# Attention's 64x64 products move from two tiles of the TensorE array to four

## The chip, the cores and the metric

The kernel runs on one core of one Trainium2 chip. The metric is the device time of that core in microseconds (us), from one launch, as the median of several runs. Five engines matter: PE is the matrix engine TensorE (PEld its weight loads), DVE VectorE, ACT ScalarE, POOL GpSimd, and SP issues the DMAs. PSUM is the memory into which TensorE writes. It has 8 banks of 128 partitions x 512 float32 values.

## The reference, cut to what matters

Attention runs inside chunks of 64 tokens, for 8 heads of dimension 64. Its output, with the heads put side by side, is the input of a gated layer, whose output is the input of a second layer.

```python
B, H, S, D = 8, 8, 576, 64           # 4608 tokens, H * D = 512 features
# q_c, k_c, v_c: (B, H, 9, 64, 64), chunks of 64 tokens
scores = np.matmul(q_c, k_c.transpose(0, 1, 2, 4, 3)) / np.sqrt(D)
attn = np.exp(scores - scores.max(-1)) ; attn /= attn.sum(-1) + 1e-09
x = np.matmul(attn, v_c)             # then (4608, 512)
y = (silu(x @ w_gate) * (x @ w_val)) @ w_out          # 512 -> 1536 -> 512
h = y @ w_in                                          # 512 -> 2048
out = (h * sigmoid(1.702 * h)) @ w_out2               # 2048 -> 512
```

## The kernel before, in words

**Tokens.** The 4608 tokens are 9 blocks of 512, and a block is 4 units of 128 tokens. A unit is two chunks of 64 tokens by 8 heads, so 16 small attention problems, 36 units in all.

**Passes.** Four passes go over the 9 blocks: two for the gated layer (half of its features each), two for the second layer. In pass 0 the attention of later units is computed between the products of the current block: while block b is multiplied, the attention of block b+1 is made ready. Units 0 to 3 come before everything else, units 4 to 7 go one by one (function `attend`), and units 8 to 35 are pipelined (`attend_next`): one PE step holds the value products of unit u-2 and then the score products of unit u.

**One unit.** `blocks` (L631) computes 16 products of 64x64 in float32, on 64 partitions each: rows 0 to 63 of the operands give rows 0 to 63 of the output, rows 64 to 127 give rows 64 to 127. Each such product stands in the trace as two pairs of a weight load and a matmul. So a set of 16 products is 32 pairs, and a unit has two sets, one for the scores (`s<-k,q`) and one for the values (`a<-e,v`). Between them stand the softmax (L670 the maximum, L671 the subtraction, both DVE reading the scores from PSUM; L673 the exponential on ACT; L674 to L678 sum and division on DVE) and four 128x128 transposes (L687), copied back by ACT (L690). `attended` copies the value products to `xr` (and, for block 0, also splits them into a high part and a low part, `x`, with ACT and DVE).

**Other products.** The layers multiply in three float32r matmuls each (`mm3`, L386 to L388), 128 rows by 128 columns with 256 or 512 moving columns. The first matrix product of a group is done in seven block products instead of eight, save in the first block (`group_plain`).

**PSUM.** The tags are `ya`, `yb` (two banks each) and `ga`, `gb`, `s`, `a` (one each), eight banks in all. `s` holds a unit's scores. `a` holds in turn its transposes and its value products. In pass 0 the products of the layers use `ga`, `gb`, `ya`, `yb`.

**Order.** No loop order decides what stands next to what: `Program` records every operation with a planned cost in us, a priority and its buffers, runs a list scheduler over them (with rounds that move priorities to due times) and emits the instructions of each engine in the order found. So a changed cost or dependency can move instructions anywhere. The weights come as 64-bit words and are converted on ACT and DVE (L456 to L464) and split (L370, L379) during pass 0, among them those of the later passes.

Of the kernel before, what the change touches and what calls it, by code (L numbers as in the profile page):

```python
# [20 lines left out]
P = 128  # L21
CH = 64
# [6 lines left out]
class Buf:  # L29
# [3 lines left out]
    def __init__(self, make, prev=None, before=None, whole=None):  # L33
        self.make, self.prev, self.before, self.whole, self.bank = make, prev, before, whole, False
        self.users, self.writers, self.openers, self.next, self.tile = [], [], [], None, None
# [18 lines left out]
class Ring:  # L54
    banks = None

# [3 lines left out]
    def new(self, shape, dtype=F32):  # L60
        def make():
            return self.pool.tile(shape, dtype, tag=self.tag, name=self.tag, bufs=self.bufs)

        prev = self.made[-self.bufs] if len(self.made) >= self.bufs else None
        b = Buf(make, prev, self.made[-1] if self.made else None)
        b.bank = self.pool is self.banks
        if prev is not None:
            prev.next = b
        self.made.append(b)
        return b  # L70
# [7 lines left out]
class Program:  # L78
# [15 lines left out]
    def op(self, eng, us, fn, reads=(), writes=(), prio=0, table=None, near=None, port=None):  # L94
# [7 lines left out]
        for b in writes:  # L102
            deps.update(b.users)
            if not b.users:
                if b.prev is not None:
                    deps.update(b.prev.users)
                    list(b.line())[-1].openers.append(o)
                if b.before is not None and b.before.tile is None:
                    follows.add(b.before.users[0])
        for b in (*reads, *writes):  # L110
            for a in b.line():
                a.users.append(o)
                for w in a.next.openers if a.next is not None else ():
                    w.deps.add(o)
                    w.follows.discard(o)
# [158 lines left out]
def attention_two_moe_kernel(ctx: ExitStack, tc: tile.TileContext, q, k, v, wg, wv, wo, wi, wo2, out):  # L274
# [51 lines left out]
    Ring.banks = pool["ps"]  # L326
    ring.update({tag: Ring(pool["ps"], tag, 1) for tag in ("ya", "yb", "ga", "gb", "s", "a")})
# [196 lines left out]
    def combos_from_quarters(j, g, prio):  # L524
# [3 lines left out]
        w3 = Buf(lambda: e.ap, e, None, e.whole)  # L528
# [110 lines left out]
    def unit(u, bufs=None, both=None):  # L639
# [3 lines left out]
        un.both = None  # L643
        if both is None:
            un.s = ring["s"].new([P, 512])
        else:
            un.both = ring[both].new([P, 2, 512])
            un.s = un.both.part(lambda ap: ap[:, 0])
        return un

    def in_a(un):
        return ring["a"].new([P, 512]) if un.both is None else un.both.part(lambda ap: ap[:, 1])

    def scores(un, prio, done=None):

        if done is None:
            op("pe", 1.24, lambda: blocks(un.s.ap, un.q.ap, un.k.ap), [un.q, un.k], [un.s], prio)
        else:
# [5 lines left out]
            attended(done, prio)  # L664

    def softmax(un, prio):
        s, e = un.s, un.e
        m = ring["m"].new([P, H, 1])
        z = ring["z"].new([P, H, 1])
        op("dve", 0.67, lambda: nc.vector.tensor_reduce(out=m.ap, in_=heads(s.ap), axis=AX.X, op=ALU.max), [s], [m], prio)  # L670
        op("dve", 0.68, lambda: nc.vector.tensor_tensor(  # L671
            out=heads(e.ap), in0=heads(s.ap), in1=m.ap.to_broadcast([P, H, CH]), op=ALU.subtract), [s, m], [e], prio)
# [8 lines left out]
    def turned(un, prio):  # L681
        pt, e = in_a(un), un.e
# [8 lines left out]
        un.o = in_a(un) if un.both is None else pt  # L691

    def attended(un, prio):
# [4 lines left out]
        if b == 0:  # L698
            n = un.u // 2
            if n not in X0:  # L700
                X0[n] = [ring["x"].new([P, KD, HT], F32R) for _ in range(2)]
            th = slice(un.u % 2 * P, un.u % 2 * P + P)
            split(*[x.part(lambda ap: ap[:, :, th]) for x in X0[n]], un.o, 512, prio, "dve",
                  lambda ap: ap.rearrange("p (a t) -> p a t", a=NP))
        copy(xr[b].part(lambda ap: ap[:, :, ts]), un.o, 512, prio, cut=lambda ap: ap.rearrange("p (a t) -> p a t", a=NP))

    def alone(un, prio):
        op("pe", 1.24, lambda: blocks(un.o.ap, un.v.ap, un.e.ap), [un.v, un.e], [un.o], prio, near=1.0)
# [108 lines left out]
    def group_products(g, xs, at, put, p):  # L817
# [3 lines left out]
        bank = [ring[t].new([P, 2, HT]) for t in (("s", "a") if p and n_groups[0] % 2 else ("ga", "gb"))]  # L821
# [33 lines left out]
    def group_plain(g, xs, at, put):  # L855
        n_groups[0] += 1
        bank = [ring[t].new([P, 2, HT]) for t in ("ga", "gb")]
# [44 lines left out]
    def group_gated(g, xs, at, put, early, apart):  # L902
# [61 lines left out]
        z = ring["ga"].new([P, 2, HT])  # L964
        bank = {label: ring[alone[label]].new([P, 2, HT]) if label in alone else z for label in ORDER[2]}
# [32 lines left out]
    def o_banks():  # L998
        ya, yb = [ring["y" + i].new([P, 2, 2, 256]) for i in "ab"]
        one = [ring[t].new([P, 2, 256]) for t in ("gb", "s", "a")]  # L1000
# [3 lines left out]
    def o_sum(p, b, label, banks, kept, prio):  # L1004
# [19 lines left out]
        m = banks[label]  # L1024
# [13 lines left out]
        elif label == "7":  # L1038
# [3 lines left out]
            if final:  # L1042
                tt(c, c, u3, ALU.add, 512, prio, "pool")
                tt(c, c, banks["5"], ALU.add, 512, prio)
            else:
                tt(c, u3, banks["5"], ALU.add, 512, prio)
            out_quarter(3, c)
            tt(u2, u2, banks["5"], ALU.add, 512, prio)
            tt(u3, u3, banks["4"], ALU.subtract, 512, prio)
# [38 lines left out]
    warm = ring["ya"].new([P, 2, 512])  # L1088
# [29 lines left out]
    for u in range(UPB):  # L1118
# [4 lines left out]
        attend(u, -40 + 4 * u, -60+3*u, bufs, (None, None, "yb", "ya")[u])  # L1123
# [166 lines left out]
```

## Time and profile before

| what | value |
|---|---|
| median of 3 runs | 1705.27 us (1704.3 to 1705.37) |
| the profiled execution's own time | 1703.92 us |
| its span in the profile | 1701.9 us |
| PE busy in the span | 1685.2 us (99%) |
| DVE, ACT, POOL busy | 1105.5, 887.1, 730.1 us |
| mean DMA rate | 278 GB/s |

The span runs from the first instruction of the program to the end of the last. About 2 us of the execution's time lie outside it. Busy time is the union of an engine's instructions. Matmuls overlap in the pipeline, so the distance from one start to the next says what a matmul costs, not its duration.

### The profile page before, as it was taken

To read this page: it belongs to the slowest core of one execution; us is meant where nothing else is said; L and a number is where in the kernel's file an instruction comes from. 1 tells how busy PE (TensorE), PEld (TensorE's weight loads), DVE (VectorE), ACT (ScalarE), POOL (GpSimd) and SP (SyncE) were. 2 spreads that over 40 slices of the span, in tenths; PEclk is the share of its full clock that TensorE was granted. 3 is DMA by queue.
4 is the path that set the end of the run, shared out by engine and by line. 5 is a ranking of instruction groups with operands and counts; after the bars stand their busy time and mean duration, and the time that the engine had idled before them with its cause. 6 is when DMAs were issued, how large, how long until landed. Compare 5 with 4: busy or idle time off the path is not lost.

```text
span 1701.9 us, 36408 instructions
## 1 busy us (share of the span) xinstructions
PE 1685.2 (99%) x14428; PEld 1609.8 (95%) x14428; DVE 1105.5 (65%) x1606; ACT 887.1 (52%) x1505; POOL 730.1 (43%) x736
## 2 busy tenths in 40 slices
PE   8999999999999999999999999999999999999998
PEld 7989999899999999999999999999999999999998
DVE  7878777787773664455454477887855556655555
ACT  7967766676643543333333456655544444444443
POOL 2595645565663464121211235667741133333333
PEclk9999999999999999999999999999999999999999
DMA  7668888888889988667779998999989977777773
GB/s 294 195 240 283 279 280 303 285 278 296 294 280 372 311 299 285 240 233 248 246 250 321 378 344 291 312 320 316 329 258 327 358 234 227 231 234 237 233 250 119
DMA packets 184154, 472.66 MB, mean 278 GB/s; under 512 B 19760, under 2 KB 44848, under 8 KB 183728
## 3 DMA queue, kind: packets, MB, share of 16 engines
q1 hardware_dynamic: 183984, 470.34, 81.2%
q8 instruction: 114, 1.87, 0.5%
q14 instruction: 56, 0.46, 0.1%
HBM read 331.84 MB, written 138.41 MB: 276 GB/s over the span
## 4 chain that ended last, share of the span: by engine, by line
PE 93%; DVE 2%; issue 1%; DMA 1%; ACT 1%; POOL 0%; POOLq 0%; DVEq 0%; ACTq 0%; SPq 0%
PE ga L386 11%; PE ga L388 11%; PE ga L387 11%; PE ya L386 5%; PE yb L388 5%; PE ya L388 5%; PE yb L386 5%; PE yb L387 5%; PE ya L387 5%; PE gb L386 4%; PE gb L388 4%; PE gb L387 4%; PE s L386 2%; PE s L388 2%; PE s L387 2%; PE a L386 2%
## 5 line engine op out<-in xcount | busy, mean ns | idle before, releaser
L370 ACT COPY u<-ga 128x512 f32<-128x512 f32 x222 | 129.8, 585 | 200.2 <-PE ga L388 199.3
L379 DVE TENSOR_TENSOR c<-u,ga 128x512 f32<-128x512 f32 x140 | 95.7, 684 | 173.2 <-PE ga L388 164.9
L386 PE MATMUL ga<-x,wc 128*128 128x256 f32 x728 | 207.7, 285 | 0.4
L387 PE MATMUL ga<-x,wc 128*128 128x256 f32 x728 | 205.5, 282 | 0.0
L388 PE MATMUL ga<-x,wc 128*128 128x256 f32 x728 | 205.4, 282 | 0.0
L924 ACT ACTIVATE xr<-c 128x512 f32<-128x512 f32 x136 | 86.0, 632 | 148.3 <-DVE c L379 146.8
L386 PEld LDWEIGHTS ga<-x,wc 128*128 128x128 f32 x728 | 138.3, 190 | 6.9 <-ACT u L370 3.1
L387 PEld LDWEIGHTS ga<-x,wc 128*128 128x128 f32 x728 | 138.5, 190 | 3.2
L388 PEld LDWEIGHTS ga<-x,wc 128*128 128x128 f32 x728 | 138.8, 191 | 0.0
L386 PE MATMUL ga<-x,wa 128*128 128x256 f32 x488 | 138.3, 283 | 0.0
L387 PE MATMUL ga<-x,wa 128*128 128x256 f32 x488 | 137.6, 282 | 0.0
L388 PE MATMUL ga<-x,wa 128*128 128x256 f32 x488 | 137.6, 282 | 0.0
L379 DVE TENSOR_TENSOR c<-u,gb 128x512 f32<-128x512 f32 x116 | 79.2, 682 | 87.7 <-ACT u L370 74.3
L379 POOL TENSOR_TENSOR u<-u 128x512 f32<-128x512 f32 x36 | 48.2, 1340 | 176.4 <-ACT u L370 176.4
L379 POOL TENSOR_TENSOR k<-xr,q 128x512 fp32r<-128x512 f32 x24 | 32.1, 1338 | 209.6 <-ACT q L370 181.2
L386 PE MATMUL ga<-x,wb 128*128 128x256 f32 x424 | 119.8, 283 | 0.6 <-ACT u L370 0.6
L388 PE MATMUL ga<-x,wb 128*128 128x256 f32 x424 | 119.7, 282 | 0.0
L387 PE MATMUL ga<-x,wb 128*128 128x256 f32 x424 | 119.6, 282 | 0.0
L379 DVE TENSOR_TENSOR xr<-xr 128x512 f32<-128x512 f32 x136 | 106.3, 782 | 11.1 <-ACT xr L924 9.2
L884 ACT ACTIVATE h<-c 128x512 f32<-128x512 f32 x102 | 63.8, 631 | 90.5 <-DVE c L379 87.8
L379 DVE TENSOR_TENSOR hl<-h,hh 128x512 fp32r<-128x512 f32 x108 | 84.6, 783 | 25.1 <-ACT hh L370 22.9
L379 DVE TENSOR_TENSOR h<-h,c 128x512 f32<-128x512 f32 x102 | 87.2, 858 | 20.9 <-ACT h L884 19.5
(335 smaller groups left out, 6224.3 us busy)
## 6 DMA issues: line engine op xcount, KB each, us to landing
x<-x_dram SPq DMA_DIRECT2D x182, 512.0 KB, 5.4
o<-od_b SPq DMA_DIRECT2D x119, 512.0 KB, 4.6
o<-od_a SPq DMA_DIRECT2D x102, 512.0 KB, 5.1
x_dram<-x SPq DMA_DIRECT2D x56, 512.0 KB, 5.4
wd_b<-ws SPq DMA_DIRECT2D x56, 256.0 KB, 4.4
od_b<-ws SPq DMA_DIRECT2D x56, 256.0 KB, 4.5
raw<-in_moe_w_out SPq DMA_DIRECT2D x44, 255.8 KB, 4.9
wd_a<-ws SPq DMA_DIRECT2D x42, 256.0 KB, 4.7
```

The lines of the kernel that those rows point to most:

```text
L370: op("act", act_us(n), lambda: nc.scalar.copy(out=dst.ap, in_=cut(src.ap)), [src], [dst], prio, near=near)
L379: lambda: e.tensor_tensor(out=dst.ap, in0=of_a(a.ap), in1=of_b(b.ap), op=by), [a, b], [dst], prio, near=near)
L386: nc.tensor.matmul(o, ah, bh, start=first, stop=False, **kind)
L387: nc.tensor.matmul(o, ah, bl, start=False, stop=False, **kind)
L388: nc.tensor.matmul(o, al, bh, start=False, stop=last, **kind)
L884: op("act", act_us(512), lambda h=h, i=i: nc.scalar.activation(out=h.ap, in_=of(0)(c[i].ap), func=AF.Silu), [c[i]], [h], prio, "silu")
L924: op("act", act_us(512), lambda: nc.scalar.activation(out=h.ap, in_=c.ap, func=AF.Gelu_apprx_sigmoid), [c], [h], prio, "gelu")
```

## The change

Four things change together.

- **Four tiles.** The 16 products of a set run over four combinations of operand rows (0 to 63, 64 to 127) and output rows (0 to 63, 64 to 127) instead of two. For the scores the operand rows are chosen by head parity and the output rows by the chunk. Products from different operand rows go to different banks, since both may write the same output rows. `score_blocks` and `value_blocks` go round the four tiles in the order (0,0), (1,1), (0,1), (1,0).
- **Banks.** The eight banks are one tile `banks`, cut by the class `Banks`, which tracks users bank by bank. A unit's scores take the left half (256 columns) of two banks, mostly those of `s` and `a`, and the value products of the unit before take the right half of the same two banks. The four transposes fill the second of the two banks, as before. In the first block unit 1 uses the banks of `ga` and `gb`.
- **Host layout.** The host lays q and k out by head parity, and permutes the rows of `w_gate` and `w_val` to match the new order of x's features. No work is added on the chip for that.
- **Planner.** The planned cost of one set falls from 1.24 to 0.8 us, that of two from 2.2 to 1.3, the time planned for attention in a block from 13 to 8 us, and units 4 to 7 get earlier priorities.

```diff
+class Banks:
+    HOME = {"ya": (0, 2), "yb": (2, 2), "ga": (4, 1), "gb": (5, 1), "gab": (4, 2), "s": (6, 1), "a": (7, 1), "sa": (6, 2)}
...
+        b = Buf(make, list(dict.fromkeys(a for a in self.last[first:first + n] if a is not None)))
...
-            t += sum(step_us(g) for g in gs) + (13.0 if p == 0 and b < NB - 1 else 0) + (3 * GV if p == b == 0 else 0)
+            t += sum(step_us(g) for g in gs) + (8.0 if p == 0 and b < NB - 1 else 0) + (3 * GV if p == b == 0 else 0)
...
-    def blocks(o, st, mv):
-        for i in range(H):
-            for r in (slice(0, CH), slice(CH, P)):
-                cs = slice(i * CH, i * CH + CH)
-                nc.tensor.matmul(o[r, cs], st[r, cs], mv[r, cs], start=True, stop=True)
+    def quads(places):
+        for g in range(H // 4):
+            for c in range(2):
+                for a, b in ((0, 0), (1, 1), (0, 1), (1, 0)):
+                    yield places(g, c, a, b)
+
+    def score_blocks(un):
+        for g, c, a, b in quads(lambda g, c, a, b: (2 * g + c, b, a, b)):
+            cs = h64(2 * g + b)
+            nc.tensor.matmul(un.s.ap[h64(b), a, h64(g)], un.q.ap[h64(a), cs], un.k.ap[h64(a), cs], start=True, stop=True)
+
+    def value_blocks(un):
+        for g, c, a, b in quads(lambda g, c, a, b: (g, c, a, b)):
+            cs = h64(2 * (2 * g + b) + c)
+            nc.tensor.matmul(un.o.ap[h64(b), a, h64(2 * g + c)], un.v.ap[h64(a), cs], un.e.ap[h64(a), cs],
+                             start=True, stop=True)
...
     def scores(un, prio, done=None):
+        t = two(un)
+        un.s = left(t)
         if done is None:
-            op("pe", 1.24, lambda: blocks(un.s.ap, un.q.ap, un.k.ap), [un.q, un.k], [un.s], prio)
+            op("pe", 0.8, lambda: score_blocks(un), [un.q, un.k], [un.s], prio)
         else:
+            done.o = right(t)
             def both_blocks():
-                blocks(done.o.ap, done.v.ap, done.e.ap)
-                blocks(un.s.ap, un.q.ap, un.k.ap)
-            op("pe", 2.2, both_blocks, [done.v, done.e, un.q, un.k], [done.o, un.s], prio, near=1.0)
+                value_blocks(done)
+                score_blocks(un)
+            op("pe", 1.3, both_blocks, [done.v, done.e, un.q, un.k], [done.o, un.s], prio, near=1.0)
...
-        pt, e = in_a(un), un.e
+        pt, e = two(un).part(lambda ap: ap[:, 1]), un.e
...
-            attend(UPB + u, t + 4 + u * 16, t - 6 + u * 16)
+            attend(UPB + u, t + 0 + u * 14, t - 10 + 0 + u * 14, None, "sa")
```

Three places show how the instructions moved. The first is PE's order at the program's start, with the score products of units 0 to 3 (L631 before, L662 now), the transposes (L687, L732), the value products (L667 now) and single matmuls on `ident` that only keep PE busy (L1096, L1146). Before:

```order
L631 MATMUL s<-k,q 64x64 x16
L1096 MATMUL ya<-ident 128x128 x6
L631 MATMUL yb<-hl,hh 64x64 x16
L631 MATMUL s<-hl,hh 64x64 x16
L1096 MATMUL ya<-ident 128x128 x4
L687 MATMUL a<-ident,e 128x128 x4
L1096 MATMUL ya<-ident 128x128 x10
L631 MATMUL a<-e,v 64x64 x16
L631 MATMUL ya<-hl,hh 64x64 x16
L631 MATMUL s<-k,q 64x64 x16
```

And now:

```order
L662 MATMUL banks<-k,q 64x64 x16
L1146 MATMUL banks<-ident 128x128 x2
L662 MATMUL banks<-hl,hh 64x64 x16
L1146 MATMUL banks<-ident 128x128 x2
L662 MATMUL banks<-hl,hh 64x64 x16
L1146 MATMUL banks<-ident 128x128 x10
L732 MATMUL banks<-ident,e 128x128 x4
L1146 MATMUL banks<-ident 128x128 x6
L667 MATMUL banks<-e,v 64x64 x16
L732 MATMUL banks<-ident,c 128x128 x4
```

The counts of products are the same. Units 1 and 2 still come early, but unit 4's scores (the last row of before) have moved behind the first products of the layer.

The second place is DVE in the same stretch, up to the second of the two subtractions that give the low part of x for units 2 and 3 (`x<-ya,x` before, the second `x<-banks,x` now); `t` and `wc` are weights under conversion, L678 and L723 the last step of unit 4's softmax. Before:

```order
L678 TENSOR_TENSOR e<-e,z 128x512
L379 TENSOR_TENSOR h<-h,gb 128x256
L461 SCALAR_TENSOR_TENSOR wc_365<-wc_365,wb_268 128x512 x2
L379 TENSOR_TENSOR h<-h,ga 128x256
L464 SCALAR_TENSOR_TENSOR wc_365<-wb_268,wc_365 128x512 x2
L379 TENSOR_TENSOR x<-yb,x 128x4x128
L461 SCALAR_TENSOR_TENSOR t<-t,wa_318 128x512
L464 SCALAR_TENSOR_TENSOR t<-wa_318,t 128x512
L379 TENSOR_TENSOR x<-ya,x 128x4x128
```

And now:

```order
L399 TENSOR_TENSOR h<-h,banks 128x256
L481 SCALAR_TENSOR_TENSOR wc_358<-wc_358,wb_273 128x512 x2
L484 SCALAR_TENSOR_TENSOR wc_358<-wb_273,wc_358 128x512 x2
L719 TENSOR_REDUCE z<-e 128x8
L720 TENSOR_SCALAR z<-z 128x8
L399 TENSOR_TENSOR x<-banks,x 128x4x128
L722 RECIPROCAL z<-z 128x8
L723 TENSOR_TENSOR e<-e,z 128x512
L399 TENSOR_TENSOR h<-h,banks 128x256
L481 SCALAR_TENSOR_TENSOR t<-t,wa_318 128x512
L484 SCALAR_TENSOR_TENSOR t<-wa_318,t 128x512
```

The second subtraction has moved ahead of the conversion of `t`, of the second `h` and of the end of unit 4's softmax.

The third place is DVE at a pipelined unit in block 2 of pass 0 (unit 13), between the maximum of its scores (L670, now L715) and the subtraction (L671, now L716), with the block sums `xt` of the next block's x between them. Before:

```order
L670 TENSOR_REDUCE m<-s 128x8
L379 TENSOR_TENSOR xt<-xr 128x512
L752 TENSOR_TENSOR xr<-xr 128x2x256
L379 TENSOR_TENSOR xt<-xr,xt 128x512
L671 TENSOR_TENSOR e<-s,m 128x512
L379 TENSOR_TENSOR xt<-xt,xr 128x512
```

And now:

```order
L715 TENSOR_REDUCE m<-banks 128x8
L716 TENSOR_TENSOR e<-banks,m 128x2x4x64
L399 TENSOR_TENSOR xt<-xr 128x512
L802 TENSOR_TENSOR xr<-xr 128x2x256
L399 TENSOR_TENSOR xt<-xr,xt 128x512
L399 TENSOR_TENSOR xt<-xt,xr 128x512
```

The subtraction now follows the maximum at once. That holds for 32 of the 36 units, and for 26 before. Of the ten others of before, five pipelined units have three instructions in between, as here.

## Rows read from the trace of the kernel before

**Rows 1.** The page's busy line by engine, and its 40 slices.

```profile
PE 1685.2 (99%) x14428; PEld 1609.8 (95%) x14428; DVE 1105.5 (65%) x1606; ACT 887.1 (52%) x1505; POOL 730.1 (43%) x736
...
PE   8999999999999999999999999999999999999998
```

**Rows 2.** Busy time by stretch: PE, PEld, DVE, ACT, POOL, PE clock, DMA share, GB/s.

```profile
0.00:40.40 40.40, 33.33 (x486) 30.68 (x486) 30.64 (x51) 28.38 (x47) 9.11 (x14) 0.92 0.81 300
40.40:60.00 19.60, 19.60 (x185) 18.15 (x186) 18.91 (x26) 17.20 (x28) 10.64 (x7) 1.00 0.65 215
60.00:80.00 20.00, 20.00 (x230) 18.74 (x227) 16.33 (x28) 18.67 (x30) 10.69 (x8) 1.00 0.50 164
80.00:98.20 18.20, 18.20 (x211) 15.53 (x209) 13.34 (x16) 14.03 (x23) 14.80 (x10) 1.00 0.59 198
98.20:482.00 383.80, 382.02 (x3940) 353.00 (x3938) 298.53 (x468) 259.98 (x434) 226.76 (x256) 1.00 0.84 283
```

**Rows 3.** The same view, a stretch of pass 1.

```profile
500.00:600.00 100.00, 100.00 (x691) 92.83 (x690) 50.09 (x78) 42.37 (x76) 38.94 (x52) 1.00 0.95 338
```

**Rows 4.** PE's waits, whole span: total us, times, longest.

```profile
PE gb L387 <- DVE x L379: 2.3, 2, 1.5
...
PE ya L386 <- DVE yv L374: 0.7, 1, 0.7
```

**Rows 5.** PE timeline around one pipelined step: start, duration, count.

```profile
150.09 1.15 PE L631 MATMUL a<-e,v 64*64 64x64 f32 x32
151.08 1.10 PE L631 MATMUL s<-k,q 64*64 64x64 f32 x32
152.11 0.38 PE L386 MATMUL ga<-x,wa 128*128 128x256 f32 x1
```

**Rows 6.** PE timeline around one set that stands alone.

```profile
51.94 1.15 PE L631 MATMUL s<-k,q 64*64 64x64 f32 x32
53.02 0.50 PE L386 MATMUL yb<-hh,o 128*128 128x512 f32 x1
```

**Rows 7.** Line L631 from 95 to 490 us: count, duration ns min/median/max.

```profile
L631 PEld LDWEIGHTS a<-e,v x896: 129/135/135, 96.2 to 481.4; 64*64 64x64 f32 x180
L631 PE MATMUL a<-e,v x896: 218/218/267, 96.2 to 481.5; 64*64 64x64 f32 x180
...
L631 PE MATMUL s<-k,q x832: 218/218/218, 97.2 to 451.8; 64*64 64x64 f32 x167
```

**Rows 8.** Groups by line from 48 to 490 us.

```profile
L631 PE MATMUL a<-e,v 64*64 64x64 f32 x992 | 35.5, 221 | 0.0
L631 PE MATMUL s<-k,q 64*64 64x64 f32 x960 | 33.2, 218 | 0.0
```

**Rows 9.** PE timeline in the start, before the layer's second half block.

```profile
38.53 0.39 PE L386 MATMUL gb<-x,wb 128*128 128x256 f32 x1 [0.34 <-ACT x L370]
40.39 0.39 PE L387 MATMUL gb<-x,wb 128*128 128x256 f32 x1 [1.47 <-DVE x L379]
```

**Rows 10.** DVE timeline just before that.

```profile
36.27 1.78 DVE L461 SCALAR_TENSOR_TENSOR t<-t,wa 128x512 int32<-128x512 f32 x1
38.09 1.65 DVE L464 SCALAR_TENSOR_TENSOR t<-wa,t 128x512 int32<-128x512 int32 x1
39.66 0.68 DVE L379 TENSOR_TENSOR x<-ya,x 128x512 fp32r<-128x512 f32 x1
```

**Rows 11.** Unit 13: PE timeline, then DVE timeline.

```profile
135.68 1.10 PE L631 MATMUL s<-k,q 64*64 64x64 f32 x32
139.63 0.60 PE L687 MATMUL a<-ident,e 128*128 128x128 f32 x4
...
136.88 0.68 DVE L670 TENSOR_REDUCE m<-s 128x8 f32<-128x512 f32 x1
140.39 0.68 DVE L671 TENSOR_TENSOR e<-s,m 128x512 f32<-128x512 f32 x1
```

**Rows 12.** Unit 12: PE timeline, then DVE timeline.

```profile
122.38 1.10 PE L631 MATMUL s<-k,q 64*64 64x64 f32 x32
...
125.63 0.60 PE L687 MATMUL a<-ident,e 128*128 128x128 f32 x4
...
124.25 0.69 DVE L671 TENSOR_TENSOR e<-s,m 128x512 f32<-128x512 f32 x1
```

More of the change, by code (lines that the diff above doesn't have):

```diff
@@ L62, in make, with __init__, new @@
             return self.pool.tile(shape, dtype, tag=self.tag, name=self.tag, bufs=self.bufs)
-        prev = self.made[-self.bufs] if len(self.made) >= self.bufs else None
+        prev = [self.made[-self.bufs]] if len(self.made) >= self.bufs else []
         b = Buf(make, prev, self.made[-1] if self.made else None)
-        b.bank = self.pool is self.banks
-        if prev is not None:
-            prev.next = b
+        for a in b.prev:
+            a.next.append(b)
         self.made.append(b)
+        return b
+class Banks:
+    HOME = {"ya": (0, 2), "yb": (2, 2), "ga": (4, 1), "gb": (5, 1), "gab": (4, 2), "s": (6, 1), "a": (7, 1), "sa": (6, 2)}
+    def __init__(self, tile):
+        self.tile, self.last = tile, [None] * 8
+    def new(self, tag, shape):
+        first, n = self.HOME[tag]
+        def make():
+            ap = self.tile[:, first:first + n].rearrange("p b c -> p (b c)")
+            return ap.rearrange("p (a b c) -> p a b c", a=shape[1], b=shape[2]) if len(shape) == 4 else \
+                ap.rearrange("p (a b) -> p a b", a=shape[1])
+        b = Buf(make, list(dict.fromkeys(a for a in self.last[first:first + n] if a is not None)))
+        b.bank, self.last[first:first + n] = True, [b] * n
+        for a in b.prev:
+            a.next.append(b)
         return b
@@ L112, in op @@
                 a.users.append(o)
-                for w in a.next.openers if a.next is not None else ():
-                    w.deps.add(o)
-                    w.follows.discard(o)
+                for n in a.next:
+                    for w in n.openers:
+                        w.deps.add(o)
+                        w.follows.discard(o)
         for b in writes:
@@ L642, in unit @@
         un.q, un.k, un.v, un.e = bufs or [ring[t].new([P, 512]) for t in "qk"] + [None, ring["e"].new([P, 512])]
-        un.both = None
-        if both is None:
-            un.s = ring["s"].new([P, 512])
-        else:
[L647 to L656, printed above, removed]
-            op("pe", 1.24, lambda: blocks(un.s.ap, un.q.ap, un.k.ap), [un.q, un.k], [un.s], prio)
-        else:
+        un.both = None if both is None else banks.new(both, [P, 2, 512])
@@ L659, in both_blocks, with two, left, right @@
+        return un
+    def two(un):
+        return un.both or banks.new("sa", [P, 2, 512])
+    def left(t):
+        return t.part(lambda ap: ap[:, :, :256])
+    def right(t):
+        return t.part(lambda ap: ap[:, :, 256:])
+    def scores(un, prio, done=None):
+        t = two(un)
+        un.s = left(t)
+        if done is None:
+            op("pe", 0.8, lambda: score_blocks(un), [un.q, un.k], [un.s], prio)
+        else:
+            done.o = right(t)
             def both_blocks():
-                blocks(done.o.ap, done.v.ap, done.e.ap)
@@ L820, in group_products @@
         n_groups[0] += 1
-        bank = [ring[t].new([P, 2, HT]) for t in (("s", "a") if p and n_groups[0] % 2 else ("ga", "gb"))]
+        bank = [banks.new(t, [P, 2, HT]) for t in (("s", "a") if p and n_groups[0] % 2 else ("ga", "gb"))]
         c = [ring["c"].new([P, 2, 2, HT]) for _ in range(2)]
@@ L856, in group_plain @@
         n_groups[0] += 1
-        bank = [ring[t].new([P, 2, HT]) for t in ("ga", "gb")]
+        bank = [banks.new(t, [P, 2, HT]) for t in ("ga", "gb")]
         hs = {i: ring["h"].new([P, 2, HT]) for i in (1, 0)}
@@ L963, in group_gated @@
         alone = {"2": "gb", "3": "s", "4": "a"} if early else {}
-        z = ring["ga"].new([P, 2, HT])
-        bank = {label: ring[alone[label]].new([P, 2, HT]) if label in alone else z for label in ORDER[2]}
+        z = banks.new("ga", [P, 2, HT])
+        bank = {label: banks.new(alone[label], [P, 2, HT]) if label in alone else z for label in ORDER[2]}
         for i, label in enumerate("1263745" if early else ORDER[2]):
```

85 lines of the change are left out of this document (49 added, 36 removed).

## The prediction, made before the changed kernel was run

> **What bounds the kernel now.** I read the page first: PE is busy 99% of the span, and no slice between the first and the last is below nine tenths [rows 1]. That alone says little, since overlapping matmuls can look busy while they wait. So I read PE's waits next: the largest group in the whole trace is 2.3 us in two waits, both in the start, and the largest of those behind the start is 0.7 us [rows 4]. PE is the bound, and what a step costs on PE is what it costs the kernel, as long as the others keep up. The view by stretch tells where that could end: in the stretch that holds most of the attention, from 98.2 to 482 us, DVE works 298.5 of 383.8 us (78%), ACT 68%, POOL 59%, and the DMA engines are 84% busy; between 40.4 and 98.2 us ACT is busy 49.9 and DVE 48.6 of 57.8 us; before 40.4 us PE itself has gaps [rows 2]. The granted clock is 1.00, the 2.4 GHz level, everywhere behind the start [rows 2].
>
> **The products themselves.** A pipelined step (values, then scores) runs from 150.09 us to the next matmul at 152.11: 2.02 us for two sets [rows 5]. A set alone takes 51.94 to 53.02: 1.08 us [rows 6]. So a further set costs 0.94 us, and 0.14 us goes once per step into the switch. A set is 32 pairs of load and matmul on two tiles, 16 pairs on each, so a tile needs 0.94 / 16 = 59 ns for a pair. Each instruction lasts far longer (load 135 ns, matmul 218 ns [rows 7]): loads and matmuls of one tile already overlap, and 59 ns is a tile's own pace.
>
> With four tiles each has 8 pairs. If they run beside each other at that pace, a set takes 8 x 59 = 0.47 us, and saves 0.47 us. That is the lower bound: the number of instructions stays the same, and a tile does not become faster. The upper one is 0.94 us, nothing saved. The trace does not show four tiles, nor a pace below 29 ns per pair. I take 0.47 us, because the row it is nearest to is the one of two tiles, where the second tile costs nothing: 59 ns is what one tile's stream of 64 columns needs, while a load and a matmul of both tiles fit into it.
>
> What speaks against it: the trace shows two tiles that share neither operand rows nor output rows, and the new ones share both. The Trainium skill, "TensorE: Matmul & The Clock Gate", Part 3 (The mechanism), says that a weight load overlaps matmuls in flight only when its row group differs; by that rule the two tiles on the same rows would take turns and a set would stay at 0.94 us. The trace contradicts it in its strict form: with a load of 135 ns and a matmul of 218 ns on one tile every 59 ns, loads do run beside matmuls of the same rows [rows 7]. The rule's case comes back among the rivals.
>
> Number of sets: 896 + 832 matmuls from 95 us on [rows 7], by 32, are 54 sets, and 992 + 960 from 48 us on [rows 8] are 61. All 36 units have 72, so 11 fall before 48 us. The 54 save 54 x 0.47 = 25.4 us. They lie on the path, since PE hardly waits there.
>
> **The first 96 us.** The 7 sets between 48 and 95 us would save 3.3 us, and the 11 of the start 5.2 us, but the start waits for others: PE does one matmul of the second half block at 38.53 us, then waits for DVE until 40.39 [rows 9]. DVE comes late because the conversion of `t` takes 1.78 and 1.65 us right ahead of the subtraction that PE needs [rows 10]. In the new order this conversion stands behind it, so the subtraction can come some 3 us earlier; the bounds are 0 and 4.5 (the 3.4 us, and what else has moved behind). What is late next is the conversion itself: it and the rest have to be done in the 57.8 us that follow, of which ACT fills 49.9 already [rows 2]. If PE's stretch shrinks by 3.3 us and takes 3 us of deferred ACT and DVE work, ACT fills 53 of 54.5 us. So of 3 + 3.3 us I count 4, with bounds 0 and 8.
>
> **What is added.** The scores of one unit and the values of another now share both banks. So the transposes of the unit before, which fill the second bank, wait until DVE has read the new scores; before, they waited for the copy of the values alone. Behind a waiting transpose stands everything on PE, in order. At unit 12 the subtraction ended at 124.94 us and the transposes began at 125.63: no wait [rows 12]. At unit 13 it ended at 141.07 us, 1.44 us after the transposes had begun [rows 11]; with the old order that would now be a stall. In the new order the subtraction follows the maximum at once in 32 of 36 units, as at unit 12. I count 1 us for the whole pass, with bounds 0 and 5 x 1.44 = 7 us (the five pipelined units where three instructions stood between). The value copies and the softmax read as many elements as before, from two banks instead of one: no row shows such a read, and since DVE and ACT have slack of 22% and 32% there, I count nothing for it; an extra 0.1 us on each of the 4 readers of a unit would be 0.4 us per unit hidden in that slack. One tile for all banks adds no instruction. The host's layouts cost nothing here. The loads of q, k and v for units 4 to 7 get earlier places in SP's queue; the DMA engines are 50 to 65% busy between 40.4 and 98.2 us [rows 2], so I count nothing for what stands behind them, and if that cover is gone it falls under the bounds of the first 96 us. Behind 482 us the products and their order are the same but for a few rows at the passes' seams: nothing.
>
> **The sum.** 25.4 + 4 - 1 = 28.4 us. The profiled execution took 1703.9 us, which gives 1675.5; the median of the runs is 1.35 us above it, so 1677 us for the median.
>
> **The rivals.**
>
> *Another engine takes over.* PE needs 25 us less from 98 to 482 us, and the others have the same work in 358 us: DVE 83%, POOL 63%, DMA 90%. For it: conversions for later passes are squeezed into a shorter pass, and DVE's queue is in order. Against it: DMA at 95% went with a PE that did not wait [rows 3], and DVE at 96% with PE fully busy too (18.91 of 19.60 us) [rows 2]. A loss of a third to two thirds of the gain gives 1684 to 1693 us.
>
> *The pairs can't be issued that fast.* Four tiles need a pair every 15 ns, and 29 ns is the shortest sustained distance in the trace. If issue ends in the middle, at 22 ns, a set takes 0.70 us, 54 sets save 13 us, and with 2 us from the start the time is 1690 us (1684 to 1700). The Trainium skill, "TensorE: Matmul & The Clock Gate", Part 1 ("Wait — 56ns, not 53.3ns?"), has a floor of about 25 ns from start to start of matmuls; an estimate from that page is 0.80 us for a set and 8 us of gain. No run here shows that floor.
>
> *The change doesn't do what it says.* Tiles on the same operand rows take turns, each pair of them at 59 ns: a set stays at 0.94 us, and only the start's new order is left, 0 to 3 us: 1702 to 1706 us. For it: no row has two such tiles. Against it: the overlap of loads and matmuls within one tile.
>
> *Slower: the transposes wait for the softmax.* If DVE were late at each of the 26 pipelined steps as at unit 13, by 1.44 us, that would be 37 us against a gain of 28.4: 1714 us. It decides from 28.4 / 26 = 1.1 us a step on. Against it stands the new order on DVE.
>
> **How the numbers follow.** As forecast: 0.65, with a range of its own of 1668 (the start's 11 sets and its 4.5 us gained as well) to 1684 (nothing from the start, 4 us of waits). Another engine: 0.15. Issue: 0.08. No overlap: 0.07, most of it within 0.2% of the time, which is 3.4 us and about what a measurement of this kernel tells from no change. Slower: 0.05. So faster by over 0.2% has 0.65 + 0.15 + 0.08 + 0.01 = 0.89, within it 0.05, slower 0.06. From 1668 to 1693 us lie nearly all of the first two cases and half of the third, about 8 in 10.
>
> **What would show it.** Right: two sets in a row take about 1.08 us from the first start to the next product's, one alone 0.61; PE stays at 99%; the end of the attention moves from 482 to about 454 us; and from there on the two traces run in parallel. The start's wait for DVE ends near 37 us. Wrong: sets of 0.7 us or more with PE busy (issue, or turns); waits of PE at the transposes that DVE's subtraction ends; waits of PE at the products for weights or x, ended by DMA, DVE or ACT, between 98 and 454 us.

## The result and the profile after

| | before | after |
|---|---|---|
| median of 4 runs | 1704.78 us | 1689.22 us |
| lowest to highest | 1703.23 to 1705.37 | 1686.83 to 1689.54 |
| span of the profiled execution | 1701.9 us | 1687.2 us |

The ratio is 0.9907, with a 95% interval of 0.989 to 0.9924. The changed kernel is 15.6 us faster; forecast were about 28. The time lies inside the range, and in the stretch that the forecast gave to the first rival.

**The products.** PE's timeline of the changed kernel around a pipelined step, and around a set alone:

```profile
111.02 0.69 PE L667 MATMUL banks<-e,v 64*64 64x64 f32 x32
111.54 0.65 PE L662 MATMUL banks<-k,q 64*64 64x64 f32 x32
112.12 0.39 PE L406 MATMUL banks<-x,wb 128*128 128x256 f32 x1
...
48.49 0.69 PE L662 MATMUL banks<-k,q 64*64 64x64 f32 x32
49.12 0.39 PE L406 MATMUL banks<-x,wb 128*128 128x256 f32 x1
```

Two sets take 112.12 - 111.02 = 1.10 us where they took 2.02 [rows 5], one takes 0.63 where it took 1.08 [rows 6]. So a set costs 0.47 us instead of 0.94, and four tiles run beside each other at the pace of one. For 72 sets that is 33.6 us less work on PE, yet its span is only 14.7 us shorter. Of the other 18.9 us, 12.4 are more idle time of PE. The other 6.5 are busy time that did not shrink with the work: PE's busy time fell by 27.1 us, from 1685.2 [rows 1] to 1658.1.

**Where PE waits.** The page's busy line, then PE's waits in the whole span (total us, times, longest):

```profile
PE 1658.1 (98%) x14428; PEld 1579.5 (94%) x14428; DVE 1098.8 (65%) x1606; ACT 892.2 (53%) x1511; POOL 726.0 (43%) x736
```

```profile
PE banks L732 <- DVE c L723: 4.0, 2, 3.6
PE banks L406 <- ACT u L390: 3.5, 5, 1.4
PE banks L406 <- ACT x L390: 2.4, 1, 2.4
...
PE banks L662 <- ACT xr L390: 1.4, 1, 1.4
```

PE was idle for 16.7 us of the span before (1701.9 - 1685.2 [rows 1]), and is now for 29.1. By stretch (PE, PEld, DVE, ACT, POOL, clock, DMA, GB/s):

```profile
0.00:37.80 37.80, 27.92 (x417) 25.42 (x417) 26.32 (x46) 25.08 (x40) 5.79 (x12) 0.91 0.79 299
37.80:60.00 22.20, 20.23 (x192) 18.97 (x193) 19.02 (x27) 18.74 (x32) 13.58 (x9) 0.92 0.54 179
60.00:80.00 20.00, 19.72 (x211) 17.59 (x213) 16.48 (x26) 19.47 (x32) 11.61 (x8) 1.00 0.51 171
80.00:98.50 18.50, 16.66 (x197) 13.16 (x189) 11.21 (x14) 12.86 (x21) 18.42 (x14) 1.00 0.61 194
98.50:160.00 61.50, 56.92 (x713) 52.14 (x712) 53.77 (x80) 45.86 (x74) 36.70 (x32) 1.00 0.76 270
160.00:466.00 306.00, 304.38 (x3327) 278.56 (x3325) 236.22 (x376) 211.98 (x346) 150.04 (x177) 1.00 0.82 280
```

Against [rows 2] two things stand out. The added idle time is in the first 160 us; from there to the end of the attention it is 1.6 us. And in two of the stretches ahead of 98.5 us another engine is nearly full: ACT with 19.47 of 20 us from 60 to 80 (18.67 before), POOL with 18.42 of 18.5 from 80 to 98.5, where it had 14.80 of 18.20.

**One mark in both.** The first product of block 1 has the same layer products ahead of it on PE in every version. PE's timeline of the kernel before, and of the changed one:

```profile
98.19 0.38 PE L386 MATMUL ga<-x,wa 128*128 128x256 f32 x1
```

```profile
98.47 0.28 PE L406 MATMUL banks<-x,wa 128*128 128x256 f32 x1
99.87 0.39 PE L407 MATMUL banks<-x,wa 128*128 128x256 f32 x1 [1.12 <-POOL x L399]
```

The first 98 us brought nothing. Before, 20 sets (18.8 us) lie ahead of this mark; now 17 sets (8.0 us). So PE had 10.8 us less to do and was there no sooner. From the mark to the end of the last value products it took 383.5 us before (to 481.7) and 367.5 now (to 466.0): 16.0 us are gained there. The remainder took 1220.2 us and takes 1221.2.

Ahead of the mark PE's idle time rose from 7.1 to 14.0 us, and its busy time fell by only 6.6 us (91.1 to 84.5). One reason for the second number is the granted clock. PE had waited 2.36 us for ACT at 36.69 us and 0.83 us for DVE at 37.91. Behind these waits the clock fell to its lower level, 1.2 GHz, for most of the next 4 us, where the kernel before was at 2.4 GHz (1.00). The view by stretch of the changed kernel (the clock is the third number from the end):

```profile
38.00:40.00 2.00, 2.00 (x11) 2.00 (x12) 1.11 (x2) 1.99 (x5) 0.59 (x1) 0.57 1.04 430
40.00:42.00 2.00, 2.00 (x12) 2.00 (x12) 1.40 (x2) 2.00 (x4) 2.00 (x2) 0.57 0.18 74
```

Products of 256 columns start 0.21 us apart there (39.05 and 39.27 us) and 0.12 us apart behind it (42.25 and 42.37 us). From these numbers the fall cost about 1.5 us, an estimate. Both kernels have another such stretch between 20 and 30 us (a clock of 0.66 in both).

The mark's own product waits for nothing, it follows PE's products ahead of it. But the product behind it came at 98.41 us before and comes at 99.87 now. What ended last ahead of that one is shown by the chain of waits of the changed kernel:

```profile
78.52 1.15 POOL o L399
...
81.32 3.80 POOL wc L399 x3
...
87.70 1.61 POOL raw L399
89.32 3.41 POOL ws L399 x2
...
93.91 2.98 POOL wc L399 x2
96.89 1.70 POOL wb L399
98.59 1.24 POOL x L399
...
99.87 0.39 PE banks L407
```

From 81.32 us on POOL works through twelve weight splits without a gap, and the low part of block 1's x stands behind them in its queue. In the kernel before eight splits stood there, from 84.59 us on. The `o` split that opens the chain had waited 3.06 us for a cast by ACT.

**A wait that the shared banks brought.** PE's timeline at 93 us, then ACT's:

```profile
93.19 0.40 PE L408 MATMUL banks<-hh,o 128*128 128x512 f32 x1
94.95 0.34 PE L662 MATMUL banks<-k,q 64*64 64x64 f32 x8 [1.36 <-ACT xr L390]
...
93.80 0.61 ACT L390 CAST wb<-ws 128x512 fp32r<-128x512 f32 x1
94.32 0.58 ACT L390 COPY xr<-banks 128x512 f32<-128x512 f32 x1
```

The scores of unit 8 wait until ACT has copied the values of unit 7 out of the same two banks. Before, scores and values had a bank each.

### The profile page after: what moved, and what is told of

It is laid out like the page before. It is cut to its first block, busy times and chain, and to the rows that moved or that the text cites. A ratio compares the mean times of both kernels' runs of the same rounds, so it can differ in the third digit from the quotient of the medians.

```text
span 1687.2 us, 36353 instructions
## 1 busy us (share of the span) xinstructions
PE 1658.1 (98%) x14428; PEld 1579.5 (94%) x14428; DVE 1098.8 (65%) x1606; ACT 892.2 (53%) x1511; POOL 726.0 (43%) x736
## 4 chain that ended last, share of the span: by engine, by line
PE 84%; DVE 4%; DMA 3%; ACT 3%; issue 2%; POOL 2%; SPq 0%; POOLq 0%; DVEq 0%; ACTq 0%
PE banks L406 28%; PE banks L408 27%; PE banks L407 27%; PE banks L667 1%; DMA od_b<-ws 1%; DVE c L399 1%; PE banks L662 1%; DMA raw<-in_moe_w_out 1%; DVE xt L399 1%; DVE t L481 1%; PE banks L732 1%; ACT L718 0%; POOL ws L399 0%; DMA raw<-in_moe_w_in 0%; POOL wc L399 0%
## 5 line engine op out<-in xcount | busy, mean ns | idle before, releaser
L399 DVE TENSOR_TENSOR c<-u,banks 128x512 f32<-128x512 f32 x312 | 213.2, 683 | 307.4 <-PE banks L408 192.2
L406 PE MATMUL banks<-x,wc 128*128 128x256 f32 x1044 | 297.5, 285 | 3.2 <-ACT u L390 2.9
L407 PE MATMUL banks<-x,wc 128*128 128x256 f32 x1044 | 294.6, 282 | 0.0
L408 PE MATMUL banks<-x,wc 128*128 128x256 f32 x1044 | 294.5, 282 | 0.0
L390 ACT COPY u<-banks 128x512 f32<-128x512 f32 x261 | 152.9, 586 | 248.4 <-PE banks L408 247.2
L406 PE MATMUL banks<-x,wb 128*128 128x256 f32 x744 | 213.3, 287 | 4.2 <-ACT x L390 2.4
L406 PE MATMUL banks<-x,wa 128*128 128x256 f32 x744 | 211.3, 284 | 2.1 <-DVE c L399 1.6
L407 PE MATMUL banks<-x,wb 128*128 128x256 f32 x744 | 211.5, 284 | 0.8 <-DVE x L399 0.8
L408 PE MATMUL banks<-x,wb 128*128 128x256 f32 x744 | 211.4, 284 | 0.0
L407 PE MATMUL banks<-x,wa 128*128 128x256 f32 x744 | 210.0, 282 | 1.1 <-POOL x L399 1.1
L406 PEld LDWEIGHTS banks<-x,wc 128*128 128x128 f32 x1044 | 198.3, 190 | 13.2 <-ACT u L390 6.0
L408 PE MATMUL banks<-x,wa 128*128 128x256 f32 x744 | 210.0, 282 | 0.0
L407 PEld LDWEIGHTS banks<-x,wc 128*128 128x128 f32 x1044 | 198.4, 190 | 6.5
L408 PEld LDWEIGHTS banks<-x,wc 128*128 128x128 f32 x1044 | 198.9, 191 | 0.0
L406 PE MATMUL banks<-hh,o 128*128 128x512 f32 x432 | 173.5, 402 | 0.3 <-ACT hh L390 0.3
L408 PE MATMUL banks<-hh,o 128*128 128x512 f32 x432 | 172.6, 400 | 0.0
L407 PE MATMUL banks<-hl,o 128*128 128x512 f32 x432 | 170.8, 395 | 0.2 <-DVE hl L399 0.2
L406 PEld LDWEIGHTS banks<-x,wb 128*128 128x128 f32 x744 | 142.7, 192 | 11.2 <-ACT x L390 2.5
L407 PEld LDWEIGHTS banks<-x,wb 128*128 128x128 f32 x744 | 142.8, 192 | 5.3 <-DVE x L399 1.0
L406 PEld LDWEIGHTS banks<-x,wa 128*128 128x128 f32 x744 | 141.0, 190 | 6.8 <-DVE c L399 2.8
L407 PEld LDWEIGHTS banks<-x,wa 128*128 128x128 f32 x744 | 140.9, 189 | 4.7 <-POOL x L399 1.7
```

The source lines that it names most:

```text
L390: op("act", act_us(n), lambda: nc.scalar.copy(out=dst.ap, in_=cut(src.ap)), [src], [dst], prio, near=near)
L399: lambda: e.tensor_tensor(out=dst.ap, in0=of_a(a.ap), in1=of_b(b.ap), op=by), [a, b], [dst], prio, near=near)
L406: nc.tensor.matmul(o, ah, bh, start=first, stop=False, **kind)
L407: nc.tensor.matmul(o, ah, bl, start=False, stop=False, **kind)
L408: nc.tensor.matmul(o, al, bh, start=False, stop=last, **kind)
```

## The experiments

The lost 13 us had three candidate causes. *New waits*: the shared banks make readers and writers wait for each other, whenever PE arrives. *Late engines*: before some 100 us the other engines can't deliver sooner, and saved PE time becomes waiting. *Plan*: the planner's new numbers made a worse order. Each run was compared with the kernel before on its own chip (1704.1 to 1705.7 us there). The changed kernel's 1689.22 us is from one launch, so a difference to it holds only as far as two launches agree; the kernel before moved by 1.6 us between launches.

**e1: two tiles at a time, all else in place.**

```diff
-        for g in range(H // 4):
-            for c in range(2):
-                for a, b in ((0, 0), (1, 1), (0, 1), (1, 0)):
-                    yield places(g, c, a, b)
+        for two_tiles in (((0, 0), (1, 1)), ((0, 1), (1, 0))):
+            for g in range(H // 4):
+                for c in range(2):
+                    for a, b in two_tiles:
+                        yield places(g, c, a, b)
```

> The changed kernel with one thing undone: a set runs its eight products on tiles (0,0) and (1,1) first and then the eight on (0,1) and (1,0), so that only two tiles have work next to each other. Banks, waits and the order of everything else are those of the changed kernel. All theories: a set goes back from 0.47 to about 0.94 us, 34 us more on PE for 72 sets. Theory new waits (the 19 us that the changed kernel's PE waits more come from waits that the shared banks and their order bring, whenever PE arrives): hardly any of that is hidden, 1714 to 1722 us. Rival late engines (in the first 160 us ACT and DVE can't deliver sooner, so that saved PE time there only becomes waiting): the 30 or so sets up to 160 us hide in the waits, 1705 to 1711 us.

Measured: 1699.98 us, ratio 0.9968 (0.9955 to 0.9981). The shared premise was wrong: PE's timeline shows a step of 142.06 - 140.56 = 1.50 us, not 2.0, and a set alone of 0.91.

```profile
140.56 0.80 PE L668 MATMUL banks<-e,v 64*64 64x64 f32 x26
141.15 0.27 PE L663 MATMUL banks<-k,q 64*64 64x64 f32 x2
141.20 0.28 PE L668 MATMUL banks<-e,v 64*64 64x64 f32 x3
...
141.32 0.80 PE L663 MATMUL banks<-k,q 64*64 64x64 f32 x27
142.06 0.51 PE L406 MATMUL banks<-hh,o 128*128 128x512 f32 x1
...
65.42 0.98 PE L663 MATMUL banks<-k,q 64*64 64x64 f32 x32
66.33 0.39 PE L406 MATMUL banks<-x,wa 128*128 128x256 f32 x1
```

The first score products start while value products are still being started: a half set on two tiles begins before the one ahead of it has finished on the other two. So 28 steps of two sets cost 0.40 us more each and 16 single sets 0.28, 16 us in all. The profiled span rose by 11.2 us, and 4.2 of these lie behind the attention, where no set runs (1225.3 us against 1221.2). Ahead of the mark 4.4 us of added work moved it by 0.8 us, to 99.31. From the mark to the end of the attention 11.2 us of added work cost 6.3. So more than half was hidden in waits that were there anyway: nearly all of it ahead of the mark, as late engines has it, and less than half behind it. That fits no theory alone.

**e10 and e11: half of the start's weight conversion left out, in the changed kernel and in the one before.** One ACT and one DVE instruction of each of the 18 weight tiles of pass 0 are not issued; the order of all others is kept.

```diff
-        op("act", conv_us(n), lambda: nc.scalar.activation(
+        op("act", conv_us(n), lambda: None if short else nc.scalar.activation(
             out=word(1).bitcast(F32), in_=raw.ap[:, :, 2], func=AF.Relu, scale=up, bias=offset.ap[:, 1:]),
...
-        op("dve", dve_us(n), lambda: nc.vector.scalar_tensor_tensor(
+        op("dve", dve_us(n), lambda: None if short else nc.vector.scalar_tensor_tensor(
             out=t.ap.bitcast(I32), in0=t.ap, scalar=-4096 * up, in1=word(1).bitcast(F32), op0=ALU.add, op1=ALU.min),
```

> The changed kernel in its own order, with half of the conversion of the 18 weight tiles of the start left out (one ACT and one DVE instruction of each, so these weights are wrong): 14 us less on ACT and 12 us less on DVE, all before about 100 us. Theory late engines (before 100 us PE waits since ACT and DVE can't deliver sooner): PE's waits there fall by 6 us or more, 1676 to 1683 us. Rival order (the waits before 100 us come from the order and the banks whatever the load): 1686 to 1689 us.

> The kernel before, in its own order, with the same half of the start's conversion left out (these weights are wrong). It is the control for the run on the changed kernel: PE waits about 15 us up to 40 us here and hardly at all from 40 to 100 us. Theory late engines: the gain is smaller than in the changed kernel, 2 to 5 us, 1700 to 1703 us. Rival order: as much here as there, or nothing in both.

Measured: 1681.66 us for the changed kernel, 7.6 us faster than with the whole conversion; 1701.42 us (ratio 0.9984, 0.9975 to 0.9994) for the kernel before, 2.7 us faster than its median beside it. The mark in PE's timeline of the first and of the second:

```profile
90.47 0.28 PE L406 MATMUL banks<-x,wa 128*128 128x256 f32 x1
```

```profile
94.30 0.38 PE L386 MATMUL ga<-x,wa 128*128 128x256 f32 x1
```

With the same order on PE, less work on ACT and DVE moves the mark by 8.0 us in the changed kernel and by 3.9 in the one before. Only a part of this is waiting: PE's idle time ahead of the mark falls by 4.2 us in the changed kernel (14.0 to 9.8, where the expectation had 6 or more) and by 1.5 in the one before (7.1 to 5.6). The other part, 3.8 and 2.4 us, is busy time, and the granted clock differs there: it is 1.00 from 37.8 to 60 us in e10, where the changed kernel had 0.92, and 1.00 from 20 to 30 us in e11's profiled execution, where the kernel before had 0.66. Late engines is borne out for the first 98 us, with a price in clock beside the waits that no theory named. How much of e11's move is the clock of that one execution is open. POOL's splits move along: they are full from 80 to 98.5 us in e10 too, with 16.07 us of work in the 20 us ahead of it instead of 11.61.

**e4 and e13: old plan numbers with the new products, and new ones with the old.** In e4 the set costs 1.24 and two 2.2 in the plan, 13 us are planned per block, and units 4 to 7 have their old priorities. In e13 the kernel before gets two of the new numbers:

```diff
-            t += sum(step_us(g) for g in gs) + (13.0 if p == 0 and b < NB - 1 else 0) + (3 * GV if p == b == 0 else 0)
+            t += sum(step_us(g) for g in gs) + (8.0 if p == 0 and b < NB - 1 else 0) + (3 * GV if p == b == 0 else 0)
...
-                            attend(UPB + u, t + 4 + u * 16, t - 6 + u * 16)
+                            attend(UPB + u, t + 0 + u * 14, t - 10 + 0 + u * 14)
```

> The changed kernel with the planner's numbers of before: 1.24 and 2.2 us for a set and for two, 13 us of attention in a block, units 4 to 7 at their old priorities. Four tiles and shared banks stay. Theory plan (the new numbers made a worse order): most of the 12 us that were missing come back, 1677 to 1682 us. Theories new waits and late engines: the order changes here and there, 1685 to 1694 us.

> The kernel before with two of the planner's new numbers alone: 8 us of attention in a block instead of 13, and units 4 to 7 at the earlier priorities. Products, banks and planned costs are those of before. Theory products (the changed kernel is faster through its products; PE is the bound of the kernel before whatever the order): 1702 to 1708 us. Rival plan (the changed kernel owes part of its gain to the numbers, since the changed kernel with the old numbers took 12 us more): 1693 to 1700 us.

Measured: 1701.29 us (0.998, 0.9969 to 0.9991) and 1708.5 us (1.0028, 1.0018 to 1.0037). So the old numbers do not give the 13 us back: with them the new products gain only 3 us, and the new numbers alone lose 4. Whether other numbers would is open; e17 below tries one. In e4 the mark comes at 103.90 us, PE waits 6.3 us for a single DVE result, and the granted clock is 0.50 from 20 to 30 us and 0.66 from 40 to 50. The products and the numbers need each other.

**e3: the value copies of units 8 to 35 on DVE instead of ACT.**

```diff
-        copy(xr[b].part(lambda ap: chunks(ap[:, :, ts])), un.o, 512, prio, cut=columns)
+        copy(xr[b].part(lambda ap: chunks(ap[:, :, ts])), un.o, 512, prio, "dve" if b > 1 else "act", cut=columns)
```

> The changed kernel with the copy of the value products to xr on DVE instead of ACT for units 8 to 35, so that one engine reads both halves of the shared banks and DVE's maximum need not wait for ACT's copy. Theory new waits: transposes and scores wait less, 2 to 4 us faster than the changed kernel, 1685 to 1687 us. Rival late engines: DVE gets 28 x 0.69 = 19 us more work and ACT 17 us less; DVE was the busier one, so no gain or a loss, 1689 to 1694 us.

Measured: 1683.46 us, ratio 0.9876 (0.9861 to 0.9891), 5.8 us below the changed kernel (5.3 by the two ratios). ACT's and DVE's timelines of the changed kernel at one unit show what it removes, and DVE's of e3 what is there instead:

```profile
139.87 0.59 ACT L390 COPY xr<-banks 128x512 f32<-128x512 f32 x1 [0.46 <-PE banks L662]
...
140.49 0.69 DVE L715 TENSOR_REDUCE m<-banks 128x8 f32<-128x512 f32 x1
```

```profile
139.82 0.69 DVE L715 TENSOR_REDUCE m<-banks 128x8 f32<-128x512 f32 x1 [0.44 <-PE banks L662]
140.43 0.68 DVE L394 COPY xr<-banks 128x512 f32<-128x512 f32 x1
```

The maximum starts as ACT's copy ends (139.87 + 0.59 = 140.46): two engines read the same banks in turn. The built program holds a wait of the maximum for ACT in 23 of the 36 units, in none before and in 3 in e3. The planner knows nothing of this wait. The view of tile `m` of the changed kernel gives DVE's idle time ahead of the maxima that ACT's copy ended (us, times); in e3 there is none:

```profile
  ACT xr L390: 23.3, 19
```

The turns go the other way too. ACT's copy waits for DVE's subtraction, and ACT then works without a gap up to its copy `u` at 157.93 us. PE waits for both copies, 1.9 us in all; ACT's timeline of the changed kernel, then PE's:

```profile
154.42 0.59 ACT L390 COPY xr<-banks 128x512 f32<-128x512 f32 x1 [1.61 <-DVE e L716]
...
155.06 0.66 PE L732 MATMUL banks<-ident,e 128*128 128x128 f32 x4 [0.46 <-ACT xr L390]
...
158.56 0.39 PE L406 MATMUL banks<-x,wc 128*128 128x256 f32 x1 [1.41 <-ACT u L390]
```

This is the clearest place behind the mark where the trace leads from a turn to a wait of PE.

**e17 and e18: is that order or chance?** e17 is the changed kernel with 8.5 us of attention per block in the plan instead of 8.0, e18 is e3 with the same 8.5.

> The changed kernel with 8.5 us of attention in a block in the plan instead of 8.0, and nothing else: how far a change in the plan alone, with no reason to be better or worse, moves the time. Theory scatter is large (the differences of 2 to 6 us of e3, e8 and e9 are such chance): 3 us or more away from the changed kernel's 1689 us. Theory scatter is small: 1687 to 1691 us.

> e3 and e17 together: the value copies of units 8 to 35 on DVE, and 8.5 us of attention in a block in the plan. It repeats the comparison of e3 with the changed kernel in another order, since e17 alone came out 3 us below the changed kernel. Theory reads in turn (ACT's copy and DVE's maximum of the shared banks hold each other up, and through them PE): 3 us or more below e17, 1683 us or less, with the missing PE waits between 100 and 480 us. Rival scatter (e3's gain was its order): 1684 to 1689 us.

Measured: 1685.94 us for e17 (0.9898, 0.9875 to 0.992; its runs reach from 1684.07 to 1692.28), 1682.71 for e18 (0.9861, 0.9844 to 0.9877). A change of the plan without a reason moves the time by 3 us, so single differences of that size prove nothing. But e3's edit gained again, 3.2 us, and the stretch from 98 to 480 us agrees both times (changed kernel and e3, e17 and e18; PE's busy time is the first number behind the length):

```profile
98.00:480.00 382.00, 375.80 (x4136) 344.15 (x4135) 302.40 (x470) 267.44 (x438) 200.31 (x218) 1.00 0.81 278
```

```profile
98.00:480.00 382.00, 379.53 (x4174) 349.60 (x4173) 319.18 (x500) 258.92 (x416) 214.48 (x230) 1.00 0.82 284
```

```profile
98.00:480.00 382.00, 376.99 (x4155) 347.56 (x4155) 305.84 (x472) 262.60 (x435) 208.00 (x228) 1.00 0.81 283
```

```profile
98.00:480.00 382.00, 380.15 (x4179) 350.69 (x4179) 318.72 (x503) 249.79 (x412) 212.81 (x239) 1.00 0.84 289
```

PE's idle time there falls from 6.2 to 2.5 us and from 5.0 to 1.9, by 3.7 and 3.2, though DVE has more to do. But e8 (below) leaves the copies on ACT, DVE waits there for ACT's copy as often, and PE is idle for 1.7 us only. The same stretch of e8, and its view of tile `m`:

```profile
98.00:480.00 382.00, 380.29 (x4169) 348.70 (x4168) 299.34 (x466) 266.37 (x433) 193.35 (x214) 1.00 0.80 278
```

```profile
  ACT xr L390: 20.5, 20
```

From the mark to the end of the attention the five runs with copies on DVE (e3, e9, e14, e15, e18) take 360.4 to 362.1 us, the changed kernel takes 367.5, e17 365.2 and e8 362.0. So the edit took away 3 to 4 us of PE's idle time in two orders, and in a third order the turns cost PE next to nothing. That the turns alone are the cause is not shown: e3 also takes work off ACT (892.2 to 880.6 us busy) and changes the order.

**e8, e9, e14, e15: other relief.** e8 pipelines units 4 to 7 (`attend_next` instead of `attend`), e9 adds e3's edit to it. In e14 POOL makes xr of units 0 to 3 as the sum of x's two parts, with e3's edit, and e15 also copies the values of units 4 to 7 by DVE:

```diff
+        if b == 0:
+            tt(made, hi, lo, ALU.add, 512, prio, "pool", of_a=rd, of_b=rd)
+        else:
+            copy(made, un.o, 512, prio, "dve" if b > 1 else "act", cut=columns)
```

> The changed kernel with units 4 to 7 pipelined like the later ones (values of one and scores of another in one step) instead of one after the other, so that the scores of a unit no longer wait until the values of the one before have been copied out of the same banks. Theory new waits: the waits of PE between 40 and 100 us fall by 2 to 5 us, 1684 to 1687 us. Rival late engines: other waits take their place, 1688 to 1691 us.

> The changed kernel with both edits that were faster by themselves: units 4 to 7 pipelined, and the copy of the value products on DVE for units 8 to 35. Theory new waits (shared banks make ACT and DVE read in turn, and hold up scores and transposes; it explains the part of the lost time behind 100 us): the two gains are in different stretches and add up, 5.7 + 2.4 us below the changed kernel, 1680 to 1682 us. Rival scatter (each new order of the planner is some us better or worse by chance): no better than the better of the two, 1683 us or more.

> The changed kernel with the value copies of units 8 to 35 on DVE (as in e3) and, for units 0 to 3, xr made by POOL as the sum of x's high and low part instead of by ACT from PSUM: 4 x 0.6 us less on ACT before 40 us, 4 x 1.3 us more on POOL, which is hardly used there, and the low part of x no longer waits for that copy. Theory late engines: 1 to 3 us below e3, 1680 to 1682 us. Rival scatter: 1682 to 1687 us.

> As e14, and the value copies of units 4 to 7 on DVE too: ACT is busy 19.5 of 20 us from 60 to 80 us in the changed kernel and DVE 16.5. Theory late engines: another 1 to 2 us below e14, 1679 to 1681 us. Rival scatter: 1682 to 1687 us.

Measured: 1686.78, 1684.12, 1687.75 and 1682.42 us (the last 0.9874, 0.9858 to 0.9891). e8's time is in the range of new waits, but not for the reason given there: PE's idle time from 40 to 100 us did not fall (5.1 us in the changed kernel, 5.4 in e8). Its mark comes 1.5 us later, and the gain lies behind it; in all it is within the scatter that e17 shows. e9 does not add up, and e14 missed: its mark comes late, at 105.47 us, against 97.50 in e15. Of these 8.0 us 3.7 are idle time of PE and 4.2 busy time, at a mean granted clock of 0.89 ahead of the mark against 0.93. None of them freed the start. e3, e15 and e18, at 1682 to 1683 us, beat the changed kernel by 6 us and can't be told from each other.

## Why the forecast was right in kind and half in size

**Right: the sets.** 0.47 us a set, on the path behind the mark. The two tiles on the same operand rows took no turns. The Trainium skill, "TensorE: Matmul & The Clock Gate", Part 3 (The mechanism), says that a weight load overlaps matmuls in flight only when its row group differs. The trace does not agree: a set would stay at 0.94 us by that rule and took 0.47. The rival of slow issue fell too, with pairs 15 ns apart in the mean (0.47 us / 32). That the time lies inside the range is owed to the room left for the first rival: the sum itself was 12 us off.

**Mis-sized: "The first 96 us", where I counted 4 us.** It measured -0.3 (98.19 to 98.47). The start's wait for DVE did end near 37.9 us, as forecast, 2.5 us sooner than at 40.39 [rows 9]; PE's timeline of the changed kernel:

```profile
36.69 0.38 PE L406 MATMUL banks<-x,wb 128*128 128x256 f32 x1 [2.36 <-ACT x L390]
37.91 0.39 PE L407 MATMUL banks<-x,wb 128*128 128x256 f32 x1 [0.83 <-DVE x L399]
```

But those 2.5 us and 10.8 us of PE work were all given back by the mark. I had seen ACT's load of 97% (53 of 54.5 us) and named the conversion as late next, yet still let 4 us through; and I left POOL out, with 81% before. It became the last in the chain. e10 shows that the load of ACT and DVE moves the mark, by waits and by the granted clock, which had no term in the sum (about 1.5 us at 38 us). That POOL's own queue order (weight splits ahead of x) adds to it is read from the trace and was not tried.

**Mis-sized: "What is added", where I counted 1 us.** From the mark to the end of the attention PE's idle time rose from 1.8 us [rows 2] to 4.6 + 1.6 = 6.2 us, 4.4 us more and inside the bound of 7. Of these 1.1 us are the wait for POOL at 99.87 us, which belongs to the start. The step that failed is the sentence on the value copies and the softmax: I gave a read from two shared banks no price because its engines had slack. The two engines take turns at these banks, and with the copies on one engine PE's idle time is 3 to 4 us less (e3 and e18). But e8 shows an order in which the turns cost PE almost nothing, so the price hangs on the order as well, and how much of it is the turns alone stays open.

**The sum redone.** From the mark on there were 52 sets of 0.94 us and are now 55 of 0.47: 48.9 - 25.9 = 23.0 us; less 4.4 us of idle time is 18.6, against 16.0 measured. So 2.6 us in that stretch are not assigned. The forecast's 25.4 us counted 54 sets from 95 us on; two of these lay ahead of the mark, and three sets have moved behind it, which makes the difference to 23.0. The remainder of the kernel gave another 1.0 us back, inside the scatter of one kernel's runs.

**The rivals.** "Another engine takes over" is what happened in size, but not where I put it: not from 98 to 482 us and not DMA, but ahead of the mark, with ACT, DVE and POOL. Its sign behind the mark did show, small: between 98 and 480 us PE's products waited 3.1 us for ACT's copies and 1.3 us for DVE. Its price was also mis-added: a third to two thirds of 28.4 us lost gives 1686 to 1696 us, not 1684 to 1693; the measured time lies in both. "Transposes wait for the softmax" did not happen behind the mark: PE's one wait at a transpose there is the 0.46 us above, and ACT's copy ended it.

## What to carry to other kernels

A saving on the bound engine counts only in the stretches in which it is the bound: place the saved instructions in the trace by stretch, and where another engine is nearly full there (ACT 97% and POOL 99.6% here), count little. A wait can cost more than its length: look at the granted clock behind it. When buffers are merged to suit one engine, count who reads them in turn now, among engines that never waited for each other. In a kernel whose order comes from a planner, costs and products have to be changed together, and a difference that a half microsecond in the plan can make is no evidence.

## What the runs showed of the hardware

Matmuls on four 64x64 tiles start four in a round, and a round takes 59 ns (0.47 us / 8), the same as a round of two; that is an average of 15 ns per pair of weight load and matmul. Products on tiles that are free start ahead of products that stand before them in the program and wait for busy tiles: in e1 two tiles at a time cost 0.59 us for a further set (1.50 - 0.91) and not 0.94. Behind PE's waits of 2.36 and 0.83 us before 38 us, the granted clock was at the 1.2 GHz level for most of the stretch from 38 to 42 us (0.57 in the mean), and products of 256 columns started 0.21 us apart instead of 0.12.
